# Attention and a mixture of experts on one core: x stored from another queue, a split moved, two scatters moved into a loop

## The chip, the core and the metric

The kernel runs on one core of a Trainium2 chip. A core has five engines with instruction streams of their own: TensorE (PE, matrix products), VectorE (DVE), ScalarE (ACT), GpSimd (POOL) and SyncE (SP, which here only starts transfers), and 16 DMA engines that move data between the main memory and the on-chip memory. Each engine takes its instructions in order and waits on semaphores. The metric is the device time of one launch in microseconds (us), lower is better. A comparison of two kernels rests on their medians.

## The reference

Four batches of 5056 tokens with 256 channels go through an attention over channels (a 256 x 256 matrix for each batch), and the 20224 rows that come out go through a mixture of eight experts, of which each token takes at most one.

```python
qn = q / (np.linalg.norm(q, axis=1, keepdims=True) + 1e-06)
kn = k / (np.linalg.norm(k, axis=1, keepdims=True) + 1e-06)
s = kn.transpose(0, 2, 1) @ qn / tau          # 256 x 256 per batch
a = np.exp(s - s.max(-1, keepdims=True))
a /= a.sum(-1, keepdims=True) + 1e-09
x = (v @ a).reshape(20224, 256)

do_compute = x @ w_skip > 0                   # the others keep out = x
e_idx = argmax(x @ w_gate); gate_w = its softmax
out = x.copy()
for e in range(8):                            # tokens of expert e
    h = np.maximum(x[e] @ w1[e], 0.0)         # 256 -> 1024
    out[e] = x[e] + gate_w * (h @ w2[e])      # 1024 -> 256
```

Products are taken in a fast 32-bit format (fp32r). To keep the precision, an operand is split in a high part H (a cast, on ACT) and the rest L (a subtraction, on DVE), and the products of the parts are added up.

## The kernel before

**The stages.** The program runs through four stages.

1. From 0 to about 460 us a list of tasks written out by a planner. Tokens come in 16 chunks of up to 1280. "A" tasks load q and k and add up the scores of a chunk (`load_qk`, line 616; `scores`, line 671; squares for the norms, line 642). Behind the fourth chunk of a batch comes its softmax. "B" tasks (`attend`, lines 744 to 746) multiply a chunk of v (loaded by `load_v`, line 622, and split by `split_v`, lines 628 and 633, into vH and vL) with the attention matrix aH, aL; `keep_x` (line 751, ACT) copies each product px to the tile xo, of which there are two; `store` (lines 760 to 763) writes xo to `out`. `logits` and `route` (lines 767 to 823) find the expert and the place of each token and scatter its number into lists (line 826, POOL). "H" tasks run the first seven tiles of 512 tokens of one expert ahead, beside the attention.
2. `small.first()`: one small slot (128 tokens of one expert) is run ahead of the loops, at 461 to 473 us.
3. `large.loop()`: six iterations of two tiles of 512 tokens (lines 425 and on), at 473.7 to 752.6 us. A tile is gathered by token number (`gather_x`, line 204, POOL), goes through both products, and is scattered back into `out` (`scatter_x`, line 209, POOL; `put` calls it). The last two scatters of the last tile are `put_last()`, which stands once at the head of the loop's body, for the iteration before, and once behind the loop.
4. `keep_warm(6)`, some matmuls whose result is not used, and `small.loop()`: four iterations of two small slots (U = 2), at 756.8 to 814 us. Each slot loads 1 MB of w1 (v1r) and 1 MB of w2 (v2r) of its expert, splits w2 (`split_w2`, lines 492 and 493) and works on 128 rows. The last result is scattered behind the loop.

**What sets the order.** In stage 1 each task has an engine, a cost and a due time. The planner runs through time, and for each engine takes the ready task that is due first; what it picks is the order in which the instructions are written, and so the order on each engine. "D" tasks stand for transfers; they too occupy one modelled engine, loads by due time. `store` has two tasks there: "S" 0.06 on ACT, which writes the store, and "D" 3.7, which writes nothing and marks when xo may be taken again by a later chunk's first product.

In stages 3 and 4 the order is written by hand. A loop's body is cut into stages; `through(...)` (`behind` in the large loop) says at which point an engine has done what the stage before it promised, and `tc.stage_boundary()` is where the engines meet. So a part of an iteration on one engine may start only after the others have come through theirs. POOL's part of a small slot is: copy the row numbers `ms`, scatter the result `yo` of the slot before, copy `mc` and `mN` (lines 531 and 532), gather the rows `yg` of the next slot.

**The slot run ahead** is the same function `slot(i, u)` with i None: no stage boundaries, and its order of instructions is the order of the text. The relu of its first product is taken in two halves, g = 0 and 1 (lines 526 and 527, tiles yH and yL). It splits w2 of the other slot (v2s0) in four parts: the first two parts behind both relus, the last two within the second product (lines 543 and 544), at f == 3. Its result yo is taken from the product po at lines 552 and 553 (DVE).

Of the kernel before, what the change touches and what calls it, by code (L numbers as in the profile page):

```python
# [15 lines left out]
ALU = mybir.AluOpType  # L16
# [4 lines left out]
P = 128  # L21
B = 4
N = 5056
C = 256
NCH = 4
J = 10
TB = NCH * J
E = 8
# [115 lines left out]
def attn_moe(ctx: ExitStack, tc: tile.TileContext, q, k, vt, tau, w_skip, w_gate, w1, w2, out):  # L144
    nc = tc.nc
# [62 lines left out]
    def scatter_x(ls, src):  # L208
        i = (G.indirect_dma_start(  # L209
            out=out, out_offset=IndirectOffsetOnAxis(ap=ls[:, 0:1], axis=0),  # L210
            in_=src, in_offset=None, bounds_check=NTOK - 1, oob_is_err=False))
        apart(i, *ROWS)
        return i
# [25 lines left out]
    class Large:  # L239
# [184 lines left out]
        def loop(self):  # L424
            with tc.For_i(0, self.n, 1, iteration_sync="staggered", hint_engines=(mybir.EngineType.PE,)) as i, tc.manual_schedule():
                self.put_last()
                self.take(1)
                self.gather(1)
                load_w(self.ei, i + 1, w1, self.w1r)
                behind(G, SP)  # L430
                self.first(True)
                tc.stage_boundary()
                load_list(self.adi, i + 1, self.lN[:, :8, :], 8)
                load_w(self.ei, i + 1, w2, self.w2r)
                for t in range(4):
                    self.second(0, t)
                    if t == 1:
                        behind(T, S, V, G, SP)
                        self.transposed(1)
                tc.stage_boundary()  # L440
                self.take(0)
                self.gather(0)
                behind(G, SP)
                self.first(False)
                tc.stage_boundary()
                for t in range(4):
                    if t < 2:
                        self.split_w1(2 * t)
                        self.split_w1(2 * t + 1)
                    self.second(1, t, t < 2)  # L450
                    if t == 1:
                        self.transposed(0)
                        behind(T, S, V, G, SP)
            self.put_last()

    class Small:

# [48 lines left out]
        def slot(self, i, u):  # L506

            s = 0 if i is None else i + (u + 1)
            through = behind if i is not None else lambda *e: None
            boundary = tc.stage_boundary if i is not None else lambda: None  # L510
            o = (u + 1) % U
            load_w(self.ei, s + U, w2, self.w2r[u])
            if i is not None:
                G.tensor_copy(self.ls[o], self.lc[o])
                scatter_x(self.ls[o][:, 0, :], self.ob[o])
            through(G)
            for g in range(2):
                ph = psum["h"].tile([P, 512], F32, name="ph")
                for f in range(4):
                    po = ph[:, f * P : (f + 1) * P]  # L520
                    for kb in range(2):
                        fs = slice(kb * F + (4 * g + f) * P, kb * F + (4 * g + f + 1) * P)
                        T.matmul(po, self.w1r[u][:, fs], self.xT[u][:, kb, :], start=(kb == 0), stop=(kb == 1), skip_group_check=True)
                fs = slice(4 * g, 4 * g + 4)
                hH, hL = (h[:, fs, :].rearrange("p f t -> p (f t)") for h in (self.hH, self.hL))
                S.activation(hH, ph, AF.Relu)
                V.scalar_tensor_tensor(hL, ph, 0.0, hH, ALU.max, ALU.subtract)
                if g == 0:
                    through(T, S, V, SP)
            boundary()  # L530
            G.tensor_copy(self.lc[o], self.lN[o])
            G.tensor_copy(self.lN[o], self.lP[o])
            load_w(self.ei, s + U, w1, self.w1r[u])
            load_list(self.adi, s + (2 * U + 1), self.lP[o], 1)
            through(SP)
            gather_x(self.xg[u], self.lN[u][:, 0, :])
            through(G)
            po = psum["o", u % 2].tile([P, 512], F32, name="po")
            for c in range(2):
                self.split_w2(o, c)  # L540
            through(S, V)
            for f in range(NFB):
                T.matmul(po, self.hH[:, f, :], self.w2s[u][:, f, :, :], start=(f == 0), stop=False, skip_group_check=True)
                T.matmul(po[:, :C], self.hL[:, f, :], self.w2s[u][:, f, 0, :], start=False, stop=(f == NFB - 1), skip_group_check=True)
                if f == 3:
                    self.transposed(o)
                    for c in range(2, 4):
                        self.split_w2(o, c)
                if f == 4:
                    through(T)  # L550
            gate = self.lc[u][:, 0, 1:2].bitcast(F32)
            V.scalar_tensor_tensor(self.ob[u], po[:, C:], gate, self.xr[u], ALU.mult, ALU.add)
            V.scalar_tensor_tensor(self.ob[u], po[:, :C], gate, self.ob[u], ALU.mult, ALU.add)  # L553
# [7 lines left out]
        def loop(self):  # L561
            with tc.For_i(0, self.n, U, iteration_sync="staggered") as i, tc.manual_schedule():  # L562
                for u in range(U):
                    if u:
                        tc.stage_boundary()
                    self.slot(i, u)
            scatter_x(self.lc[U - 1][:, 0, :], self.ob[U - 1])


# [183 lines left out]
    def store(d):  # L753
        xo = xos[d]
        b, ch = divmod(d, NCH)
        r0 = b * N + ch * P * J
        r1 = r0 + 64 * J
        later = (lambda i: beside(i, "later", "ahead")) if d >= D0 else lambda i: None
        if ch < NCH - 1:
            later(nc.scalar.dma_start(out[r0 : r0 + P * J, :].rearrange("(p j) c -> p j c", j=J), xo[:, :, :C]))  # L760
        else:
            later(nc.scalar.dma_start(out[r0:r1, :].rearrange("(p j) c -> p j c", j=J), xo[0:64, :, :C]))
            later(nc.scalar.dma_start(out[r1 : r1 + 64 * (J - 1), :].rearrange("(p j) c -> p j c", j=J - 1), xo[64:128, : J - 1, :C]))

    def logits(d):
        lg[d] = pb.tile([P, J, 10], F32, name="lg", bufs=3)
# [69 lines left out]
    def tables(start):  # L836
# [15 lines left out]
            V.tensor_tensor_scan(cum[:, i, :], ones[:, :E], nsl[:, i, :], 0.0, ALU.mult, ALU.add)  # L852
        toti = tab.tile([P, 2], I32, name="toti")
        V.tensor_copy(toti[:, 0:1], cum[:, 0, E - 1 : E])
        V.tensor_scalar(toti[:, 1:2], cum[:, 1, E - 1 : E], 1.0, -1.0, ALU.max, ALU.add)
        addr, widx = [], []
        slots.extend([addr, widx, toti])
        yield
# [120 lines left out]
    for d in range(NC):  # L979
# [18 lines left out]
                sv[0][0].users = [t]  # L998
        sv[1][0].users = [t]
        lgt = read[d] = then("lg", add("V", 0.13, lambda d=d: logits(d), [s], hold=("lg", 3)))  # L1000
        st = then("st", add("S", 0.06, lambda d=d: store(d), [s], nominal["B", d, 4] + 3))
        dma = add("D", 3.7, None, [st], nominal["B", d, 4] + 16.5)
        stored[d] = dma
        g = route(d)
        r = chain(g, ("V", 0.43), deps=[lgt] + ([routed[d - 1]] if d else []))
        r += chain(g, ("S", 0.17), ("V", 0.92), ("V", 0.35), deps=r)
# [189 lines left out]
```

## Time and profile before

| | before |
|---|---|
| three runs | 818.23, 823.17, 825.82 us |
| median | 823.17 us |
| profiled execution | 822.56 us |
| its span on the core | 820.6 us |
| mean granted clock of TensorE | 0.984 |
| data moved | 144.97 MB |

The profile is of one execution. Its span is the time between the first and the last instruction that it shows; 1.96 us of the execution's own time lie around it. In a row of a timeline stand the start in us, the duration, the engine, the line of the kernel, the operation, what it writes and reads, and, in square brackets, how long the engine stood before it and what it then was released by. "q" behind an engine's name is the issue of a transfer. Rows of the table of sizes give for a stretch of time how long each engine was busy, TensorE's granted clock (1.00 is full speed), the share of time in which the DMA engines were busy, and the GB/s that they moved. Queue q1 is that of transfers started by SP, q10 of those started by ACT, q0 of those of POOL.

### The profile page before, as it was taken

To read this page: it belongs to the slowest core of one execution; us is meant where nothing else is said; L and a number is where in the kernel's file an instruction comes from. 1 tells how busy PE (TensorE), PEld (TensorE's weight loads), DVE (VectorE), ACT (ScalarE), POOL (GpSimd) and SP (SyncE) were. 2 spreads that over 40 slices of the span, in tenths; PEclk is the share of its full clock that TensorE was granted. 3 is DMA by queue.
4 is the path that set the end of the run, shared out by engine and by line. 5 is a ranking of instruction groups with operands and counts; after the bars stand their busy time and mean duration, and the time that the engine had idled before them with its cause. 6 is when DMAs were issued, how large, how long until landed. Compare 5 with 4: busy or idle time off the path is not lost. (4 is left out here: it accounts for less than half of the span.)

```text
span 820.6 us, 13438 instructions
## 1 busy us (share of the span) xinstructions
PE 787.3 (96%) x4456; PEld 695.0 (85%) x4456; DVE 514.0 (63%) x1005; ACT 365.8 (45%) x579; POOL 391.9 (48%) x423
## 2 busy tenths in 40 slices
PE   7999999979999999999999899999999999998996
PEld 6889998969998888889887778888888888887886
DVE  4719859969989563546476645646556555644665
ACT  5438657838857233325223333324233333322553
POOL 3000378868787777475576133332334433432333
PEclk9999999989999999999999989999999999999999
DMA  8979889969674151412426641222322141321886
GB/s 322 390 267 333 330 260 339 355 251 363 192 243 131 59 158 51 163 46 86 126 52 216 263 142 51 94 96 92 103 89 103 45 147 51 101 78 33 290 315 239
DMA packets 57834, 144.97 MB, mean 177 GB/s; under 512 B 14820, under 2 KB 35324, under 8 KB 52928
## 3 DMA queue, kind: packets, MB, share of 16 engines
q1 hardware_dynamic: 22464, 100.61, 33.7%
q0 software_dynamic: 13952, 22.97, 8.9%
q10 hardware_dynamic: 21376, 20.85, 8.3%
q8 instruction: 23, 0.38, 0.2%
q14 instruction: 19, 0.16, 0.1%
HBM read 114.80 MB, written 32.06 MB: 179 GB/s over the span
## 5 line engine op out<-in xcount | busy, mean ns | idle before, releaser
L826 POOL DMA_INDIRECT lst<-pay,r_posi x160 | 187.4, 1171 | 158.0 <-DVE r_posi L823 111.0
L209 POOL DMA_INDIRECT out<-xg,lc x76 | 76.5, 1006 | 167.3 <-DVE xg L345 140.0
L671 PE MATMUL s<-qt,kt 128*128 128x256 f32 x640 | 151.6, 388 | 4.3 <-DMA kt<-in_k 4.3
L671 PEld LDWEIGHTS s<-qt,kt 128*128 128x128 f32 x640 | 120.9, 195 | 20.0 <-DMA kt<-in_k 3.7
L338 PE MATMUL po<-w2s,hH 128*128 128x512 f32 x384 | 136.4, 398 | 0.0
L321 ACT ACTIVATE hH<-ph 128x512 fp32r<-128x512 f32 x96 | 57.5, 599 | 128.7 <-PE ph L318 128.7
L339 PE MATMUL po<-w2s,hL 128*128 128x256 f32 x384 | 107.2, 279 | 0.0
L744 PE MATMUL px<-aH,vH 128*128 128x266 f32 x320 | 100.0, 312 | 5.0 <-ACT xo L751 5.0
L322 DVE SCALAR_TENSOR_TENSOR hL<-ph,hH 128x512 fp32r<-128x512 f32 x96 | 66.5, 692 | 59.3 <-ACT hH L321 57.8
L204 POOL DMA_INDIRECT xg<-out,lc x80 | 85.2, 1066 | 30.4 <-issue 18.9
L745 PE MATMUL px<-aL,vH 128*128 128x266 f32 x320 | 92.7, 290 | 0.3 <-DVE aL L728 0.3
L746 PE MATMUL px<-aH,vL 128*128 128x266 f32 x320 | 92.4, 289 | 0.0
L338 PEld LDWEIGHTS po<-w2s,hH 128*128 128x128 f32 x384 | 72.1, 188 | 16.6
L751 ACT COPY xo<-px 128x532 f32<-128x532 f32 x80 | 47.7, 601 | 77.8 <-PE px L746 77.8
L316 PE MATMUL ph<-xH,w1H 128*128 128x512 f32 x192 | 76.2, 397 | 3.2 <-DVE yo L553 3.2
L338 PE MATMUL px<-w2s,hH 128*128 128x512 f32 x224 | 79.1, 396 | 0.0
L317 PE MATMUL ph<-xL,w1H 128*128 128x512 f32 x192 | 75.8, 395 | 0.0
L318 PE MATMUL ph<-xH,w1L 128*128 128x512 f32 x192 | 75.8, 395 | 0.0
L339 PEld LDWEIGHTS po<-w2s,hL 128*128 128x128 f32 x384 | 72.3, 188 | 0.5
L744 PEld LDWEIGHTS px<-aH,vH 128*128 128x128 f32 x320 | 61.2, 191 | 6.8 <-ACT xo L751 5.4
L745 PEld LDWEIGHTS px<-aL,vH 128*128 128x128 f32 x320 | 61.3, 191 | 1.9 <-DVE aL L728 0.6
L339 PE MATMUL px<-w2s,hL 128*128 128x256 f32 x224 | 62.8, 280 | 0.0
(189 smaller groups left out, 1485.1 us busy)
## 6 DMA issues: line engine op xcount, KB each, us to landing
vf<-in_vt SPq DMA_DIRECT2D x32, 640.0 KB, 5.8
qt<-in_q SPq DMA_DIRECT2D x31, 640.0 KB, 7.2
kt<-in_k SPq DMA_DIRECT2D x31, 640.0 KB, 7.9
out<-xo ACTq DMA_DIRECT2D x12, 1280.0 KB, 6.5
v1r<-in_w SPq DMA_DIRECT2D x11, 1024.0 KB, 4.9
v2r<-in_w SPq DMA_DIRECT2D x11, 1024.0 KB, 4.9
w1r<-in_w SPq DMA_DIRECT2D x7, 1024.0 KB, 4.8
w2r<-in_w SPq DMA_DIRECT2D x7, 1024.0 KB, 5.0
```

The lines of the kernel that those rows point to most:

```text
L204: apart(G.indirect_dma_start(out=to, out_offset=None, in_=out[0:n, :], in_offset=IndirectOffsetOnAxis(ap=ls[:, 0:1], axis=0), bounds_check ...
L209: i = (G.indirect_dma_start(out=out, out_offset=IndirectOffsetOnAxis(ap=ls[:, 0:1], axis=0), in_=src, in_offset=None, bounds_check=NTOK - ...
L316: T.matmul(ph, self.w1H[:, fs], self.xH[:, kb, :], start=(kb == 0), stop=False)
L317: T.matmul(ph, self.w1H[:, fs], self.xL[:, kb, :], start=False, stop=False)
L318: T.matmul(ph, self.w1L[:, fs], self.xH[:, kb, :], start=False, stop=(kb == 1))
L338: T.matmul(po, self.hH[:, f, ts], self.w2s[:, f, :, :], start=(f == 0), stop=False, skip_group_check=True)
L339: T.matmul(po[:, :C], self.hL[:, f, ts], self.w2s[:, f, 0, :], start=False, stop=(f == NFB - 1), skip_group_check=True)
L671: T.matmul(sums[b][:, cb, :], kt[:, j % JH, cb * P : (cb + 1) * P], qt[:, j % JH, :], start=(ch == 0 and j == 0 and cb == 0), stop=(ch == ...
L744: T.matmul(px[:, i, :NA], vH[:, kb, js], aH[:, kb, :], start=(kb == 0), stop=False)
L745: T.matmul(px[:, i, :NA], vH[:, kb, js], aL[:, kb, :], start=False, stop=False)
L746: T.matmul(px[:, i, :NA], vL[:, kb, js], aH[:, kb, :], start=False, stop=(kb == 1))
L826: i = G.indirect_dma_start(out=lst, out_offset=IndirectOffsetOnAxis(ap=posi[:, t : t + 1], axis=0), in_=pay[:, t0 + t, :], in_offset=None, ...
```

## The change

Four edits.

1. The stores of x are started by SP and not by ACT. In the planner the small ACT task goes, and the 3.7 "D" task writes the store, at the place in SP's order that the planner finds for it.
2. In the small slot run ahead, the four parts of the split of the other slot's w2 stand ahead of the relus: two ahead of g = 0, two ahead of g = 1. Slots in the loop keep the old places.
3. `put_last()` behind the large loop goes. It stands in the small slots' loop instead, behind the slot u = 0, and so in every iteration; the rows written are the same each time.
4. Since those scatters must run at least once, the small loop's number of slots is raised to at least one beyond the slot run ahead. With these inputs it is not changed by that.

```diff
@@ Large.loop
                     if t == 1:
                         self.transposed(0)
                         behind(T, S, V, G, SP)
-            self.put_last()
@@ Small.slot
                 fs = slice(4 * g, 4 * g + 4)
                 hH, hL = (h[:, fs, :].rearrange("p f t -> p (f t)") for h in (self.hH, self.hL))
+                if i is None:
+                    for c in range(2 * g, 2 * g + 2):
+                        self.split_w2(o, c)
                 S.activation(hH, ph, AF.Relu)
                 V.scalar_tensor_tensor(hL, ph, 0.0, hH, ALU.max, ALU.subtract)
...
             po = psum["o", u % 2].tile([P, 512], F32, name="po")
-            for c in range(2):
-                self.split_w2(o, c)
+            if i is not None:
+                for c in range(2):
+                    self.split_w2(o, c)
             through(S, V)
...
                 if f == 3:
                     self.transposed(o)
-                    for c in range(2, 4):
-                        self.split_w2(o, c)
+                    if i is not None:
+                        for c in range(2, 4):
+                            self.split_w2(o, c)
@@ Small.loop
                     self.slot(i, u)
+                    if u == 0:
+                        large.put_last()
             scatter_x(self.lc[U - 1][:, 0, :], self.ob[U - 1])
@@ store
         if ch < NCH - 1:
-            later(nc.scalar.dma_start(out[r0 : r0 + P * J, :].rearrange("(p j) c -> p j c", j=J), xo[:, :, :C]))
+            later(nc.sync.dma_start(out[r0 : r0 + P * J, :].rearrange("(p j) c -> p j c", j=J), xo[:, :, :C]))
         else:
...
@@ tables
-        V.tensor_scalar(toti[:, 1:2], cum[:, 1, E - 1 : E], 1.0, -1.0, ALU.max, ALU.add)
+        V.tensor_scalar(toti[:, 1:2], cum[:, 1, E - 1 : E], 2.0, -1.0, ALU.max, ALU.add)
@@ the tasks of a chunk
-        st = then("st", add("S", 0.06, lambda d=d: store(d), [s], nominal["B", d, 4] + 3))
-        dma = add("D", 3.7, None, [st], nominal["B", d, 4] + 16.5)
-        stored[d] = dma
+        stored[d] = then("st", add("D", 3.7, lambda d=d: store(d), [s], nominal["B", d, 4] + 16.5))
```

The last chunk of each batch has two stores, the others one: 20 in all, of up to 1280 rows of 1 KB. Line numbers behind the edits shift by two to six.

More of the change, by code (lines that the diff above doesn't have):

```diff
@@ L759, in store @@
         if ch < NCH - 1:
-            later(nc.scalar.dma_start(out[r0 : r0 + P * J, :].rearrange("(p j) c -> p j c", j=J), xo[:, :, :C]))
+            later(nc.sync.dma_start(out[r0 : r0 + P * J, :].rearrange("(p j) c -> p j c", j=J), xo[:, :, :C]))
         else:
-            later(nc.scalar.dma_start(out[r0:r1, :].rearrange("(p j) c -> p j c", j=J), xo[0:64, :, :C]))
-            later(nc.scalar.dma_start(out[r1 : r1 + 64 * (J - 1), :].rearrange("(p j) c -> p j c", j=J - 1), xo[64:128, : J - 1, :C]))
+            later(nc.sync.dma_start(out[r0:r1, :].rearrange("(p j) c -> p j c", j=J), xo[0:64, :, :C]))
+            later(nc.sync.dma_start(out[r1 : r1 + 64 * (J - 1), :].rearrange("(p j) c -> p j c", j=J - 1), xo[64:128, : J - 1, :C]))
     def logits(d):
```

## The prediction

> **What bounds the kernel now.** I read the head of the profile's page first.
>
> ```profile
> span 820.6 us, 13438 instructions
> PE 787.3 (96%) x4456; PEld 695.0 (85%) x4456; DVE 514.0 (63%) x1005; ACT 365.8 (45%) x579; POOL 391.9 (48%) x423
> PEclk9999999989999999999999989999999999999999
> q1 hardware_dynamic: 22464, 100.61, 33.7%
> q10 hardware_dynamic: 21376, 20.85, 8.3%
> ```
>
> TensorE (PE) is busy 787.3 of 820.6 us. The change does not touch the number or order of its instructions, so it can win only from two stocks: the 33.3 us in which PE stands, and stretches in which it is busy at a lower clock (the 8s in the clock row). The first stock by its causes, from the table of PE's waits:
>
> ```profile
> PE px L744 <- ACT xo L751: 5.0, 1, 5.0
> PE s L671 <- DMA kt<-in_k: 4.3, 2, 3.7
> PE ph L316 <- DVE yo L553: 3.2, 1, 3.2
> PE ph L523 <- issue: 1.5, 1, 1.5
> PE px L316 <- ACT xH L284: 1.3, 1, 1.3
> PE m L712 <- ACT r_before L805: 0.6, 1, 0.6
> ```
>
> The columns are total, count, longest. The largest is one wait of 5.0 us. Around it I read ScalarE's (ACT's) timeline and the sizes of clock and DMA share, and the store's landing times:
>
> ```profile
> 148.96 0.55 ACTq L760 DMA_DIRECT2D out<-xo  x1
> ...
> 163.29 0.61 ACT L751 COPY xo<-px 128x532 f32<-128x532 f32 x1 [0.91 <-PE px L746]
> 169.54 0.55 ACTq L760 DMA_DIRECT2D out<-xo  x1
> 170.13 1.26 ACT L628 CAST vH<-vf 128x1280 fp32r<-128x1280 f32 x1 [6.24 <-DMA kt<-in_k]
> 171.47 1.09 ACT L751 COPY xo<-px 128x532 f32<-128x532 f32 x2
> ```
>
> ```profile
> DMA to landing us min/median/max: 5.4/6.2/20.5
> ```
>
> ```profile
> 162.00:164.00 2.00, 2.00 (x19) 2.00 (x18) 2.00 (x3) 0.99 (x2) 1.39 (x3) 1.00 1.03 409
> ```
>
> ```profile
> 172.10:175.50 3.40, 3.40 (x14) 3.31 (x15) 3.16 (x10) 0.79 (x2) 1.03 (x2) 0.50 0.81 261
> 411.00:415.00 4.00, 4.00 (x13) 3.09 (x12) 1.21 (x5) 1.08 (x2) 3.09 (x4) 0.57 0.91 204
> 473.80:479.40 5.60, 5.60 (x13) 4.35 (x14) 1.29 (x2) 1.29 (x3) 1.98 (x2) 0.50 0.67 236
> ```
>
> ACT is free at 163.29 + 0.61 = 163.90, and its next instruction, a store of x, goes out only at 169.54. The table of the tile xo has one landing of 20.5 us; 148.96 + 20.5 = 169.46 is 0.08 before that issue. So I read the wait as: the new store may not be issued until the store of 148.96 has landed, and ACT, in order, holds the copies of px behind it. At 162 to 164 the DMA engines are full (share 1.03, 409 GB/s). The last fence has, as its last three columns, PE's clock, DMA share and GB/s: after the 5.0 us PE is busy 3.40 us at clock 0.50, which loses another 1.7.
>
> **The change part by part.** Sums are against the profiled execution: 822.56 us, of which 820.6 is the span. That is 0.6 below the median of 823.17; the three runs spread from 818.23 to 825.82.
>
> *Stores on SyncE (SP).* SP's row around that store, with buffer numbers: vf, qt and kt are loads, xo_1299 is the store that took 20.5 us, xo_1428 the one that waited. Before:
>
> ```order
> L622 DMA vf_1461<-in_vt 128x1280
> L616 DMA qt_1529<-in_q 128x1280
> L616 DMA kt_1530<-in_k 128x1280
> L616 DMA qt_1584<-in_q 128x1280
> L616 DMA kt_1585<-in_k 128x1280
> L622 DMA vf_1638<-in_vt 128x1280
> ```
>
> After:
>
> ```order
> L628 DMA vf_1460<-in_vt 128x1280
> L766 DMA out_0<-xo_1299 1280x1x256
> L622 DMA qt_1529<-in_q 128x1280
> L622 DMA kt_1530<-in_k 128x1280
> L622 DMA qt_1584<-in_q 128x1280
> L622 DMA kt_1585<-in_k 128x1280
> L628 DMA vf_1637<-in_vt 128x1280
> L766 DMA out_0<-xo_1428 1280x1x256
> ```
>
> The store now stands in one queue with the loads, ahead of five that competed with it. The bytes of a packet differ: 20.85 MB in 21376 packets are about 1 KB, 100.61 MB in 22464 are 4.5 KB, so beside a full load queue the store's queue moves few bytes per turn. In one queue it is served in turn. Its own packets need 4.1 us (below); with the two loads just ahead of it, 0.64 MB each at 409 GB/s and so 3.2 together, I estimate a landing of 8 to 12 us, not 20.5. ACT then never stands on a store. Gain: the whole 5.0 and the 1.7 of half clock behind it, **6.7**; the other end, nothing, is rival B.
>
> What it costs: 20 issues and the store's transfer move ahead of loads. A store of 1280 packets takes 1280/16 packets per engine at 0.083 x 820.6 x 16/21376 = 51 ns, 4.1 us; a load right behind comes that much later at most. SP also waits for xo (163.90 for xo_1428) with loads behind it. Cover: loads are early. PE waits for them twice (4.3 in the table), and both times long before the first store, by the timeline and by the first and last start of the stores:
>
> ```profile
> 3.65 2.07 PE L671 MATMUL s<-qt,kt 128*128 128x256 f32 x4 [3.65 <-DMA kt<-in_k]
> 6.38 47.97 PE L671 MATMUL s<-qt,kt 128*128 128x256 f32 x208 [0.66 <-DMA kt<-in_k]
> ```
>
> ```profile
> L760 ACTq DMA_DIRECT2D out<-xo x12: 541/552/641, 85.9 to 388.5; - x12
> ```
>
> I take 0; the other end is rival C.
>
> Two smaller places have ACT issuing two stores ahead of what PE waits for:
>
> ```profile
> 298.68 1.26 ACT L628 CAST vH<-vf 128x1280 fp32r<-128x1280 f32 x1 [1.32 <-issue]
> ```
>
> ```profile
> 408.47 0.66 ACTq L763 DMA_DIRECT2D out<-xo  x1
> 409.18 0.59 ACT L284 CAST xH<-pt 128x512 fp32r<-128x512 f32 x1 [1.32 <-issue]
> ```
>
> Each pair costs ACT 1.32. At 409 the cast of xH is what PE's 1.3 waits for; I take 1.1 of it and leave 0.2 for DVE, whose half of the split follows. Row 411 to 415 above is 4.00 us at 0.57, a loss of 4.00 x 0.43 = 1.7, which I let go too: **2.8**. The Trainium skill (TensorE: Matmul & The Clock Gate, What's actually happening) gives half rate after at least one idle window of about 3.4 us; by that a wait of 1.3 would not have lowered the clock and 1.7 could not be won here, but this trace shows half clock behind 1.3, so the trace differs and decides. At 298 the pair delays the routing chain that ends in the 0.6 wait of L712: **0.6**.
>
> *The second small slot's w2.* In DVE's row of the slot run ahead (v2s0 is the split weight of the other slot, yL the low half of the hidden layer, yo the result). Before:
>
> ```order
> L527 SCALAR_TENSOR_TENSOR yL_4797<-ph_5049,yH_4796 128x512
> L527 SCALAR_TENSOR_TENSOR yL_4797<-ph_5060,yH_4796 128x512
> L493 TENSOR_TENSOR v2s0_4794<-v2r0_4788,v2s0_4794 128x2x256 x4
> L552 SCALAR_TENSOR_TENSOR yo1_156<-po_5096,mc1_4803,yr1_4791 128x256
> ```
>
> After:
>
> ```order
> L492 TENSOR_TENSOR v2s0_4794<-v2r0_4788,v2s0_4794 128x2x256 x2
> L529 SCALAR_TENSOR_TENSOR yL_4797<-ph_5049,yH_4796 128x512
> L492 TENSOR_TENSOR v2s0_4794<-v2r0_4788,v2s0_4794 128x2x256 x2
> L529 SCALAR_TENSOR_TENSOR yL_4797<-ph_5064,yH_4796 128x512
> L556 SCALAR_TENSOR_TENSOR yo1_156<-po_5104,mc1_4803,yr1_4791 128x256
> ```
>
> Nothing stands between the last matmul and yo any more. In time:
>
> ```profile
> 470.29 0.28 PE L544 MATMUL po<-v2s,yL 128*128 128x256 f32 x1
> ```
>
> ```profile
> 470.44 1.29 DVE L493 TENSOR_TENSOR v2s<-v2r,v2s 128x512 fp32r<-128x512 f32 x2 [0.35 <-ACT v2s L492]
> 471.66 0.48 DVE L552 SCALAR_TENSOR_TENSOR yo<-po,mc,yr 128x256 f32<-128x256 f32 x1
> ```
>
> ```profile
> 465.40 0.60 ACT L526 ACTIVATE yH<-ph 128x512 fp32r<-128x512 f32 x1 [2.38 <-issue]
> ```
>
> PE ends at 470.57; L552 could start there, not at 471.66: **1.0** of PE's 3.2 goes, and the rest (L552, L553 and the entry of the large loop) stays. The casts move into ACT's 2.38 of idle time: two take 1.1, so the first relu is not delayed if the weights have landed. The half clock behind (5.60 at 0.50, 2.8 lost) may stay whole or go whole with a gap of 2.2; I let about a third go: **1.0**.
>
> *The puts.* They leave the place between the loops and enter the small loop. POOL's row, one iteration, before (between its gather and the barrier nothing stands):
>
> ```order
> L532 COPY mN1_4799<-mP1_4801 128x2
> L204 DMA yg0_153<-out_0,mN0_4798 128x256
> L562 ISA
> L514 COPY ms0_4804<-mc0_4802 128x2
> L209 DMA out_0<-yo0_155,ms0_4804 20224x256
> ```
>
> After:
>
> ```order
> L534 COPY mN1_4799<-mP1_4801 128x2
> L204 DMA yg0_153<-out_0,mN0_4798 128x256
> L209 DMA out_0<-xg1_140,lc1_148 20224x256 x2
> L566 ISA
> L513 COPY ms0_4804<-mc0_4802 128x2
> L209 DMA out_0<-yo0_155,ms0_4804 20224x256
> ```
>
> The loop runs four times here, so two puts become eight. At the entry:
>
> ```profile
> 753.80 1.57 PE L1142 MATMUL m<-ones 128*128 128x128 f32 x12 [1.26 <-PEq L425]
> 756.84 3.81 PE L523 MATMUL ph<-yT,v1r 128*128 128x128 f32 x32 [1.47 <-issue]
> ```
>
> ```profile
> 755.83 0.97 POOL L209 DMA_INDIRECT out<-xg,lc  x1 [0.31 <-DMA out<-xg,lc]
> 793.03 0.18 POOL L514 COPY ms<-mc 128x2 int32<-128x2 int32 x1 [0.75 <-DMA out<-yo,ms]
> 795.66 1.00 POOL L209 DMA_INDIRECT out<-yo,ms  x1 [2.44 <-DVE yo L553]
> ```
>
> ```profile
> 796.62 0.48 PE L543 MATMUL po<-v2s,yH 128*128 128x512 f32 x1
> ```
>
> PE finishes keep_warm at 755.37 and starts at 756.84, just behind POOL's second put (756.80): the loop's barrier waits for POOL. Without the puts I take **1.4** off. In the loop, two puts are 2 x (0.97 + 0.31) = 2.6 of POOL ahead of the COPY of 793.03, which then comes at 795.6; POOL has only 2.44 of waiting there to take them in, and the scatter follows the COPY by 0.2 at the least, so it starts between 795.8 and, with a gap like those between its other steps, 796.6; I take 796.4, 0.75 later than 795.66. The barrier behind it opens the second half of the slot for PE, which before started 0.04 before the scatter's end (796.62 against 796.66): there is no slack. So 0.75 an iteration, **+3.0** in four. The bounds come from when the second put lands, which the barrier waits for too:
>
> ```profile
> out<-xg,lc POOLq DMA_INDIRECT x76, 2.4
> out<-yo,ms POOLq DMA_INDIRECT x8, 4.3
> ```
>
> Issued at 793.03 + 1.28 = 794.3, it lands at 796.7 by its own median (no more delay) and at 798.6 by that of the loop's other scatter (2.0 an iteration, 8 in all). Nearest is its own row, so 3.0 stands; the low end is 1.5, if half of it hides. A gain is excluded: work is only added ahead of a barrier.
>
> **Sum:** 6.7 + 2.8 + 0.6 + 2.0 + 1.4 - 3.0 = 10.5. 822.56 - 10.5 = **812.1**. Own range: 807 (puts at 1.5, all of the clock at 470, a little more at the loop's entry) to 817 (puts at 8).
>
> **Rivals.**
>
> *A, half clock stays.* If it hangs on when a gap falls and not on its length, the gaps shrink and slow stretches come at other places: 1.7 + 1.7 + 1.0 are not won, 812.1 + 4.4 = 816.5. For it: 5.0, 3.2 and 1.3 all led to it. Against: behind 5.0 us no gap at all remains.
>
> *B, the landing stays 20 us.* It was full DMA engines (1.03), not the queue, and the wait goes to SP, or to the copy that reuses xo. Then the 6.7 stays: 818.8. The Trainium skill (DMA: Bandwidth & Descriptors, Issuing engines are not separate DMA queues) states this as a rule: transfers share the same engines whoever starts them, and the issuer saves only its issue time. For it: the share of 1.03. Against: the median landing is 6.2, and the slow store's 1 KB packets were in a queue of their own beside loads.
>
> *C, loads behind stores come late.* SP is in order; one or two of them arrive after PE asks, each 4.1 and a half-clock stretch of 1.7: 818 to 824. Against: PE waits for no load after the start.
>
> *D, slower: the puts' landing gates the loop.* If under the loop's loads a put takes as much longer as the slow store did (20.5/6.2 = 3.3 times 2.4 = 7.9 us), issued at 794.3 it lands at 802.2, and all engines wait 5.6 in every iteration: 812.1 + 22.4 - 3.0 = 831.5. It turns slower than before from 3.4 an iteration, a landing of 5.8. For it: no slack. Against: 4.3 for a scatter in the same loop.
>
> **How the numbers follow.** Chances: forecast 0.56, A 0.13, B 0.13, C 0.07, D 0.11. 1% is about what a measurement can tell from no change (the runs spread 0.9%); its bounds are 814.9 and 831.4. Faster by over 1%: 0.56 x 0.85, a third of A, little of B: 0.53. Slower: half of D, 0.06. Same: 0.41. The range, 806 to 822, leaves out D, part of C and the forecast's lowest tail, some 0.2.
>
> **What would show it.** Right: no ACT wait near 164 to 170, no store over some 12 us, the L744 wait gone; SP's loads without a new PE wait on kt, qt or vf; L556 starting within 0.2 of PE's end at 470; PE in the small loop within 0.5 of keep_warm's end; PE's wait before the second half of slot 0 at 0.7 to 1 in each iteration, released by POOL. Wrong: a new wait of L671 for kt, a wait on SP that holds vf, a wait in the loop that ends at a put's landing, or half clock at new places.

## The result and the profile after

The change makes the kernel slower: 826.59 us (median of 20 runs, 820.30 to 831.37) against 818.87 us (median of 20, 815.28 to 825.82), a ratio of 1.0081 with a 95% interval of 1.0057 to 1.0105. Ratios here and below are estimated from the single executions, without those over 1.5% above the fastest of their kernel, and so need not be the quotient of the medians beside them. Forecast were 812.1 us and a range of 806 to 822. The profiled execution of the kernel after took 826.61 us, its span is 825.0 us, 4.4 more than in the one of before (820.6).

The head of the page of the kernel after, the same rows as were shown of before:

```profile
span 825.0 us, 13506 instructions
PE 787.1 (95%) x4456; PEld 695.4 (84%) x4456; DVE 514.3 (62%) x1005; ACT 366.7 (44%) x579; POOL 396.2 (48%) x429
PEclk9999999999999999999999899999999999999998
q1 hardware_dynamic: 43008, 121.32, 42.0%
```

PE does as much as before; queue q1 (SP) now has the 20.7 MB that q10 (ACT) had. The table of PE's waits of the kernel after, where the first row is new:

```profile
PE po L546 <- issue: 11.5, 4, 3.8
PE s L677 <- DMA kt<-in_k: 5.5, 2, 3.9
PE ph L522 <- issue: 2.9, 1, 2.9
...
PE ph L316 <- DVE yo L557: 2.1, 1, 2.1
...
PE po L546 <- ACT yH L528: 1.6, 1, 1.6
...
PE m L718 <- ACT r_before L811: 0.6, 1, 0.6
```

The wait of 5.0 us on L744 is gone, the one for yo is 2.1 and not 3.2, and no new wait for qt, kt or vf appeared (the two for kt stand at the start, before any store). The last row, L712 in before, is the wait whose end was forecast at 0.6: it is still there. What is new stands in the small loop (L546, and L522 with 2.9 instead of 1.5).

PE's order is the same in both kernels, product for product. So the start of the same product in both traces can be taken from each other, which shows where time goes and comes (worked out from all 4456 products; minus is earlier than before):

```text
stretch of the trace of before, and what lies there    forecast   measured
165 to 180    store on ACT, 5.0 us of PE, half clock       -6.7       -7.1
245 to 255    nothing of the change                         0         +1.6
300 to 312    two stores ahead of vH                       -0.6       -1.9
406 to 418    two stores ahead of xH                       -2.8       -2.8
470 to 482    entry of the large loop                      -2.0       -2.2
752 to 761    entry of the small loop                      -1.4       +3.1
761 to 814    the small loop                               +3.0      +15.0
elsewhere                                                   0         -1.4
sum                                                       -10.5       +4.3
```

Up to the end of keep_warm the kernel after is 13.8 us ahead; it loses 18.1 from there on. The execution of before that was profiled (822.56) lay 3.7 above the median of its 20 runs.

The small loop, from the end of keep_warm to PE's last product, first before and then after, as rows of the table of sizes (PE busy, PEld, DVE, ACT, POOL, then clock, DMA share, GB/s):

```profile
755.40:814.00 58.60, 54.28 (x400) 50.08 (x400) 36.07 (x61) 30.70 (x64) 22.97 (x42) 1.00 0.83 292
```

```profile
741.60:818.30 76.70, 60.49 (x401) 55.71 (x400) 36.47 (x61) 31.49 (x64) 33.13 (x48) 0.91 0.69 240
```

58.6 us became 76.7. PE stands 16.2 instead of 4.3, and is busy 6.2 longer at a mean clock of 0.91. One iteration in POOL's timeline of the kernel after, then PE at the same place, then the group of transfers issued between 789 and 790 (the last number is the time from issue to landing):

```profile
787.71 1.14 POOL L209 DMA_INDIRECT out<-xg,lc  x1 [0.69 <-issue]
789.15 0.97 POOL L209 DMA_INDIRECT out<-xg,lc  x1 [0.30 <-DVEq L566]
791.11 0.97 POOL L209 DMA_INDIRECT out<-yo,ms  x1 [0.79 <-POOL ms L513]
795.03 0.19 POOL L533 COPY mc<-mN 128x2 int32<-128x2 int32 x1 [2.94 <-issue]
```

```profile
794.94 0.47 PE L546 MATMUL po<-v2s,yH 128*128 128x512 f32 x1 [3.81 <-issue]
```

```profile
out<-xg,lc POOLq DMA_INDIRECT x1, 5.2
```

The second put is issued at 789.15 and lands at 789.15 + 5.2 = 794.35; 0.6 later PE and POOL go on together. POOL had finished its scatter at 792.08. So it is not POOL's time that PE waits for but the put's landing. The same sum holds in the other iterations: 753.18 + 4.3 and PE at 758.15, 770.33 + 4.8 and PE at 775.71, 807.46 + 5.7 and PE at 813.70, each time 0.6 behind the landing. The scatter of yo, issued behind the puts, could be thought to be what is waited for, since it lands at about the same time in three of the iterations. The first iteration rules it out, where PE goes on at 758.15 and it lands at 755.39 + 4.3 = 759.7 (POOL, PE and the transfer issued between 755 and 757):

```profile
755.39 0.98 POOL L209 DMA_INDIRECT out<-yo,ms  x1 [0.79 <-DVE yo L557]
758.15 0.47 PE L546 MATMUL po<-v2s,yH 128*128 128x512 f32 x1 [1.59 <-ACT yH L528]
out<-yo,ms POOLq DMA_INDIRECT x1, 4.3
```

This is the second half of the slot u = 1; the prediction's list of signs calls it slot 0.

Behind three of these waits PE runs at half clock for 3.4 us, as in this row:

```profile
775.50:779.00 3.50, 3.29 (x11) 2.94 (x12) 1.29 (x2) 1.08 (x2) 2.25 (x3) 0.51 0.39 119
```

### The profile page after: what moved, and what is told of

It is laid out like the page before. It is cut to its first block, busy times and chain, and to the rows that moved or that the text cites. A ratio compares the mean times of both kernels' runs of the same rounds, so it can differ in the third digit from the quotient of the medians.

```text
span 825.0 us, 13506 instructions
## 1 busy us (share of the span) xinstructions
PE 787.1 (95%) x4456; PEld 695.4 (84%) x4456; DVE 514.3 (62%) x1005; ACT 366.7 (44%) x579; POOL 396.2 (48%) x429
## 5 line engine op out<-in xcount | busy, mean ns | idle before, releaser
L832 POOL DMA_INDIRECT lst<-pay,r_posi x160 | 184.1, 1151 | 154.7 <-DVE r_posi L829 108.3
L209 POOL DMA_INDIRECT out<-xg,lc x82 | 83.7, 1021 | 162.7 <-DVE xg L345 138.9
L677 PE MATMUL s<-qt,kt 128*128 128x256 f32 x640 | 149.5, 384 | 5.6 <-DMA kt<-in_k 5.5
L677 PEld LDWEIGHTS s<-qt,kt 128*128 128x128 f32 x640 | 118.9, 192 | 21.1 <-DMA kt<-in_k 4.4
L204 POOL DMA_INDIRECT xg<-out,lc x80 | 82.9, 1036 | 30.0 <-issue 19.2
L344 DVE SCALAR_TENSOR_TENSOR xg<-po,lc,xg 128x256 f32<-128x256 f32 x48 | 23.2, 484 | 62.1 <-PE po L339 51.3
```

Of the source, the lines that this page charges most:

```text
L204: apart(G.indirect_dma_start(out=to, out_offset=None, in_=out[0:n, :], in_offset=IndirectOffsetOnAxis(ap=ls[:, 0:1], axis=0), bounds_check ...
L209: i = (G.indirect_dma_start(out=out, out_offset=IndirectOffsetOnAxis(ap=ls[:, 0:1], axis=0), in_=src, in_offset=None, bounds_check=NTOK - ...
L677: T.matmul(sums[b][:, cb, :], kt[:, j % JH, cb * P : (cb + 1) * P], qt[:, j % JH, :], start=(ch == 0 and j == 0 and cb == 0), stop=(ch == ...
L832: i = G.indirect_dma_start(out=lst, out_offset=IndirectOffsetOnAxis(ap=posi[:, t : t + 1], axis=0), in_=pay[:, t0 + t, :], in_offset=None, ...
```

## The experiments

Three sets of runs were made, each on a chip of its own and beside runs of before there. On the chips of the first and the third set the kernel before takes 902.12 and 913.70 us, and PE stands for up to 13 us a time in the straight-line part between 100 and 560 us, from a cause that I did not find; ratios there are wide, and I read those traces by stretch. In the second set before takes 820.88 us.

**Set 1. The puts back behind the large loop (edits 1 and 2 alone).** Against the kernel after:

```diff
@@ Large.loop
+            self.put_last()
@@ Small.loop
-                    if u == 0:
-                        large.put_last()
```

(Edit 4, which only edit 3 needs, is taken back with it.)

> The kernel after, with the two scatters of the last large tile back behind the large loop (edits 1 and 2 alone). Theory: the two traces run 13.75 us apart in favour of the kernel after until the end of keep_warm (755.37 against 741.62), and all of the loss is in the small loop, through the puts. Then this kernel is faster than before by 7 to 14 us (0.985 to 0.991 of before, since the wait of 5 us in the trace of before need not be in each of its runs), and in the small loop PE waits for no landing. Rival: the small loop is slow for another reason that edits 1 or 2 bring (code placed differently, half clock): then the loop still takes over 75 us from the end of keep_warm and the time is not below that of before by 1%.

893.02 us, ratio 0.9932 (0.9886 to 0.9978): faster, and by less than the theory has it. In the trace the small loop takes 59.9 us, and PE waits for no landing in it, so the loop's loss is gone; the size came out in set 2.

**Edit 1 alone** (stores started by SP, planner's task as in the change; the rest as before).

> The kernel before with edit 1 alone: stores of x started by SyncE. Theory: the waits behind ACT's store issues go, 5 to 10 us off, ratio 0.988 to 0.994. Rival: the 20.5 us landing was an accident of the one profiled execution of before; then only the 1 to 3 us of the smaller places go, ratio 0.996 to 0.999.

894.36 us, ratio 0.9994 (0.9945 to 1.0043). By the time alone the rival is right here. By its reason it is not: at the stretch of the long landing, the same products of PE as above, less their start in the trace of before, move like this in the traces (us, from 165 to 180 of that trace):

```text
stores on ACT:  edit 3 -0.2   edit 2 -1.7, 0.0   pad on before +0.4
stores on SP:   after -7.1   edits 1, 2 -7.0, -7.1   edit 1 -7.1, -7.1   pad, edits 1, 2 -7.1
```

On every chip edit 1 wins 7 us there against the trace of before. On this one the other stalls of stage 1 sum up to over 70 us by its end, and the gain is not seen in the time: 7 us would be a ratio of 0.992, below the interval, so by the times a part of it is lost again. Where is not settled. In the next stretch, 180 to 245, the four traces of sets 1 and 3 with stores on SP lose 0.6 (this kernel), 3.2, 7.1 and 8.3 us, where the four with stores on ACT lose under 0.5. So on these chips it is not excluded that loads come late behind stores (rival C); the traces from there hold no landing of loads or stores by which it could be told.

**Edit 3 alone** (puts in the small loop, with edit 4, which they need; the rest as before).

> The kernel before with edit 3 alone: the two scatters in the small loop, in every iteration. Theory: the small loop grows by 16 to 19 us as in the kernel after (waits of 3.5 to 3.8 us in three iterations and 1.6 in one, three or four stretches of half clock of 3.4 us each, and a slower entry), ratio 1.018 to 1.023. Rival: a part of the loss comes from the other edits (the loop starts at another time, the code stands elsewhere): then under 12 us, ratio below 1.014.

916.76 us, ratio 1.0142 (1.0022 to 1.0261): the interval takes in both theory and rival, but the trace decides. The small loop takes 76.2 us from keep_warm's end, against 58.6 in before and 76.7 in the kernel after: all of the growth inside the loop comes with this edit. PE's first wait in this kernel's table:

```profile
PE po L542 <- issue: 14.6, 4, 4.0
```

The entry of the loop, though, was not slower here but faster: a gap of 0.30 us. That part of the theory fell.

This kernel has its stores on ACT and so also tells whether the long landing was an accident of one execution. ACT's timeline, and PE's:

```profile
158.12 0.56 ACTq L761 DMA_DIRECT2D out<-xo  x1
...
178.48 0.55 ACTq L761 DMA_DIRECT2D out<-xo  x1
179.08 1.26 ACT L629 CAST vH<-vf 128x1280 fp32r<-128x1280 f32 x1 [6.30 <-DMA kt<-in_k]
```

```profile
181.05 0.59 PE L745 MATMUL px<-aH,vH 128*128 128x266 f32 x1 [5.09 <-ACT xo L752]
```

The same store, the same wait, PE's 5.09 against 5.03. This trace holds no landing of the store, but the next one is issued 20.4 us behind it, against 20.6 in before. In the three other traces with stores on ACT (edit 2 alone, twice, and the pad on the kernel before, all below) PE's wait is 3.58, 5.23 and 5.36; in the nine with stores on SP there is none. The long landing belongs to the order of before, on every chip on which that order was traced.

**Edit 2 alone** (the split ahead of the relus, the rest as before).

> The kernel before with edit 2 alone: the second slot's w2 split ahead of the relus in the slot run ahead. Theory: the gap of 3.2 us at the entry of the large loop shrinks to 2.1 to 2.2 and one stretch of half clock of 3.4 us behind it goes, 2.7 us in all, ratio 0.996 to 0.998. Rival: the second stretch of half clock stays, 1.0 us, ratio 0.999. A second look at the stores started by ACT as well: theory, one of them takes over 15 us again and PE waits over 3 us for it; rival, none does.

901.93 us, ratio 1.0029 (0.9969 to 1.0088): too wide. In the trace the gap at the entry of the large loop is 2.1 us, as in the kernel after. What its stores show stands above.

**Set 2. POOL's time without a landing.**

```diff
@@ Small.loop (the kernel of the first experiment)
                     self.slot(i, u)
+                    if u == 0:
+                        for t in range(3):
+                            G.memset(large.xg[2], 0.0)
```

> The kernel of the first experiment (puts behind the large loop) with three clears of an unused tile on POOL (0.97 us each in the trace, 2.9 in all) where the loop's puts stood in the kernel after, and no transfer there. Theory: what costs 17 us in the loop is that the barrier waits for the second put's landing, not POOL's 2.6 us of issuing; then from the end of keep_warm to PE's last product the loop takes 58.6 us plus at most 0.75 x 4, so under 63, and PE waits under 1.5 us an iteration at the second half of slot 1. Rival: POOL's time is the cost; then PE waits 3 us or more there in three of four iterations and the loop takes over 70.

810.04 us, ratio 0.9841 (0.9799 to 0.9883), the same as without the clears (0.9859, the next experiment). In POOL's timeline the clears take 3.0 us at the puts' place:

```profile
766.85 1.06 POOL L204 DMA_INDIRECT yg<-out,mN  x1 [0.63 <-issue]
767.90 3.00 POOL L574 MEMSET xg<- 128x1024 f32 x3
770.85 0.19 POOL L514 COPY ms<-mc 128x2 int32<-128x2 int32 x1
771.85 1.00 POOL L209 DMA_INDIRECT out<-yo,ms  x1 [0.82 <-DMA yg<-out,mN]
```

and PE's waits inside the loop are 2.1 us in all. The loop takes 64.8, over the 63 that I set, but its entry gap is 4.8 and not 1.5, and of a stretch of half clock there (6.8 us) 5.9 lie behind it and cost 3.0; without this excess it is 58.5, as before. The rival is out: POOL has room for 3 us an iteration.

**The first experiment's kernel once more.**

> The kernel of the first experiment once more (edits 1 and 2, puts behind the large loop), for its time where the runs of before scatter less. Theory: 6 to 12 us below before, ratio 0.985 to 0.993; all of what the kernel after lost is in the loop's puts. Rival: the fetch of code at the loop's entry and the half clock behind it take back half of the gain, ratio 0.993 to 0.997.

809.85 us against 820.88, ratio 0.9859 (0.9827 to 0.9891): 11 us faster than before. The small loop in its trace, in a row of the table of sizes:

```profile
740.00:798.00 58.00, 54.52 (x401) 50.15 (x400) 36.00 (x61) 30.58 (x64) 24.19 (x42) 1.00 0.83 295
```

So edits 1 and 2 together do about what was forecast for them (6.7 + 2.8 + 0.6 + 2.0 = 12.1), and edit 3 takes it away and more.

**Code that stands elsewhere.** Twelve keep_warm matmuls ahead of everything, where PE waits for its first load:

```diff
         ran = plan.run()
+        keep_warm(12)
```

> The kernel of the first experiment with twelve matmuls of keep_warm's kind at the very start of PE's stream, where PE waits 3.65 us for its first load, so that all later code of PE stands 48 instructions (3 KB) further on. Theory: in five traces PE's entry of the small loop is late (2.7 to 4.9 us after keep_warm, where before has 1.5 and the third experiment 0.3) because a block of 16 KB of PE's code is fetched only then (at most 0.4 us before keep_warm's end, or behind it; in the two others 4.7 us before); moved by 48 instructions the block is fetched before keep_warm, the entry gap falls to 0.3 to 1.5 us and the half clock behind it goes, so 3 us less than the first experiment's kernel. Rival: the gap is the barrier of the loop itself, and stays at 2.7 or more wherever the code stands.

805.26 us, ratio 0.9791 (0.9761 to 0.9822): 4.6 us less than the kernel without them, and the fastest of all. Its six runs lie between 803.81 and 806.60, those of the other between 806.29 and 812.03. The two traces do not show the difference: in both the code was there in time, and the gap is 1.45 and 1.47. That the other runs of the kernel without the twelve had it late is inferred. The matmuls also do something that the expectation left out: with them the first products of the scores follow each other every 0.22 us, without them the first dozen or so every 0.43, which is the pace of half clock. By the 208th product that is worth 0.4 us (it starts at 52.50 and 52.88 us in the two traces), since PE waits for kt in between in both. What the loop's entry does in all traces is worked out from the transfers of kind "instruction" on queue q8 (16 KB each, PE's code) and from the duration of the branch at the head of the loop in PE's queue:

```text
kernel             puts ahead   q8 fetch, us from    branch   gap before PE's
                   of the loop  keep_warm's end      us       first product, us
before             yes          -4.7                 0.47     1.47
edits 1, 2 (set 2) yes          -4.7                 0.47     1.47
edit 3             no           -4.7                 0.47     0.30
after              no           -0.4                 2.95     2.91
edit 1 (set 1)     yes          -0.4                 1.67     2.67
edit 1 (set 3)     yes          +1.4                 3.69     4.76
edits 1, 2 (set 1) yes           0.0                 2.03     3.02
edit 2 (set 1)     yes          +1.9                 3.89     4.89
edit 2 (set 3)     yes          -0.4                 1.93     2.92
POOL's clears      yes          +1.4                 3.77     4.84
empty scatters     yes          +1.4                 3.83     4.92
pad, edits 1, 2    yes          in the large loop    0.37     1.45
pad, before        yes          in the large loop    0.36     1.43
pad, after         no           in the large loop    0.35     0.26
```

In all eight rows with a late fetch the branch ends 1.5 us behind the fetch's end, whenever that is. Where the code is there, the entry takes 1.4 to 1.5 us behind the puts and 0.3 without them; where it is fetched late, 2.7 to 4.9. The two rows of edits 1 and 2 are the same kernel, so it changes from run to run, or from chip to chip; in the three kernels with the pad (the twelve matmuls) it was in time.

**Scatters that write nothing.**

```diff
@@ Small.loop (the kernel of the first experiment)
                     self.slot(i, u)
+                    if u == 0:
+                        for t in range(2):
+                            scatter_x(self.nowhere, large.xg[1][:, 2 + t, :])
```

The tile `nowhere` holds numbers out of range.

> The kernel of the first experiment with two scatters in the loop, at the place where the kernel after has its puts, whose row numbers are all out of range, so that they write nothing (the true puts stand behind the large loop). POOL's time and the wait of the barrier are those of the kernel after, no bytes move. Theory: a landing is mostly a fixed time, so it is still 3 us or more and the loop takes 68 to 76 us from the end of keep_warm to PE's last product. Rival: the 128 KB that each put moves beside 300 GB/s of loads make the landing long; without them it lands within 2 us and the loop takes under 64.

823.79 us, ratio 1.0022 (0.9993 to 1.0052), 14 us more than without the scatters. The loop takes 78.0 us, 2 over the theory's 76, of which its late entry (4.9 and not 1.5) is 3.4, and POOL and PE stand as in the kernel after:

```profile
791.28 1.21 POOL L209 DMA_INDIRECT out<-xg,nowhere  x1 [0.30 <-issue]
793.48 0.98 POOL L209 DMA_INDIRECT out<-yo,ms  x1 [0.79 <-POOL ms L516]
797.40 0.18 POOL L536 COPY mc<-mN 128x2 int32<-128x2 int32 x1 [2.94 <-issue]
```

```profile
797.31 0.76 PE L549 MATMUL po<-v2s,yH 128*128 128x512 f32 x1 [3.24 <-issue]
```

The barrier opens 6.0 us after the issue of an empty scatter. The rival, that the bytes make the landing long, is out. What makes it long is not shown.

**Set 3. Edit 1 alone once more.**

> The kernel before with edit 1 alone (stores of x started by SyncE), once more where the runs of before scatter less. By products of PE that stand at the same place of both orders, the trace of the kernel after gains 6.9 us at the wait of 5.0, 1.3 at 303 and 3.1 at 409 and loses 1.7 to a stretch of half clock at 249: theory, edit 1 alone gives 9 to 11 us, ratio 0.986 to 0.990. Rival: in runs without a profile the long landing is rarer, and it gives under 4 us, ratio above 0.995.

915.35 us, ratio 0.9964 (0.9922 to 1.0006), so not the theory's 0.986 to 0.990 on this chip. Its 7.1 us at the stretch of the long landing are in the list above; in this trace, of an execution of 922.36 us, 8.3 are lost in the stretch behind it, and an entry gap of 4.8 us takes 3.3 more.

**Edit 2 alone once more.**

> The kernel before with edit 2 alone (second small slot's w2 split ahead of the relus), once more. Theory: 2.5 us at the entry of the large loop (1.1 of gap and one stretch of half clock of 1.7 lost, by the trace of the kernel after), ratio 0.996 to 0.998. Rival: the later or earlier fetch of code at the small loop's entry takes it back or adds to it by 3 us, so the ratio is 1.000 or 0.993.

915.14 us, ratio 0.9989 (0.9948 to 1.0031): open. The late fetch was there (2.9 us of entry gap), but its part cannot be told from the time.

**The pad on the kernel before.**

> The kernel before with twelve matmuls of keep_warm's kind at the start of PE's stream and nothing else changed. Theory: they hide in PE's wait of 3.65 us for its first load; their only other effect is that the code of the small loop's entry is there in time in every run. The profile of before had it in time, so the entry gap stays 1.5 us there; over many runs it gives 0 to 2.5 us, ratio 0.997 to 1.000. Rival: the matmuls at the start themselves win or cost something, over 3 us in either direction.

913.31 us, ratio 0.9994 (0.9961 to 1.0028). The matmuls themselves cost or win nothing that could be measured in the time here; the entry gap is 1.43 us.

**The pad on the kernel after.**

> The kernel after with the same twelve matmuls at the start. Theory: the entry gap of 2.9 us falls to 0.5 or less, since neither puts nor code are waited for there, the half clock behind it goes, and 3 to 4.5 us are won against the kernel after (ratio to before 1.003 to 1.006); the waits for the puts' landing in the loop stay at 3.5 us. Rival: the entry gap is the loop's own barrier and stays; then the ratio stays at 1.008.

933.48 us, ratio 1.0219 (1.0174 to 1.0264): neither 1.003 to 1.006 nor 1.008, on a chip where edits 1 and 2, each alone, were not seen to gain anything clear of the noise. By the trace the theory holds: the gap at the entry, and PE's wait in the loop:

```profile
846.49 1.69 PE L522 MATMUL ph<-yT,v1r 128*128 128x128 f32 x13 [0.26 <-issue]
```

```profile
PE po L546 <- issue: 15.4, 4, 4.1
```

With code in time the entry is won as forecast (0.26 against 1.43), and the puts' landing costs what it cost before.

## Why the prediction was wrong

**The stores: right.** 6.7 forecast, 7.1 measured. The longest landing in the kernel after, from the table of the tile xo, is

```profile
DMA to landing us min/median/max: 5.4/6.6/11.3
```

where 8 to 12 was estimated and 20.5 was before. Rival B and the rule of the Trainium skill that it rests on (DMA: Bandwidth & Descriptors, Issuing engines are not separate DMA queues) say that the issuer does not matter beyond the issue time. Here the move did more than that: the same 1280 rows landed after 20.5 us in a queue beside the loads, and after at most 11.3 in line with them. Whether it is the queue, or the place ahead of five loads that came with it, was not taken apart. Loads behind stores came in time in this trace (rival C out; on the chips of sets 1 and 3 it stays open).

**The smaller places: right in sum, in part by luck.** 470: 2.0 and 2.2. The wait is 2.1 to 2.3 in every trace with edit 2 and 3.1 to 3.4 in every one without; DVE's result now starts 0.03 behind PE's last product:

```profile
459.08 0.48 DVE L556 SCALAR_TENSOR_TENSOR yo<-po,mc,yr 128x256 f32<-128x256 f32 x1 [1.70 <-PE po L547]
```

409: 2.8 and 2.8. PE's wait of 1.26 goes in every trace with stores on SP, and stays at 1.26 to 1.28 in the four others with stores on ACT. But in those four no half clock follows it, so the 1.7 behind it in before was not there to be won in every run, and that it went is not the edit's doing alone. 303: 0.6 forecast, 1.9 measured, and by another way. The wait on L712 is 0.63 in all fourteen traces, so that reading of the prediction failed; what goes in the traces with stores on SP is a wait of 0.56 on L282 just behind it. The rest is a stretch of half clock that I had left out, and it hangs little on the edit: it is gone in two traces with stores on ACT, and there in two with stores on SP. One such stretch came up at a new place (239.7, behind a wait of 1.65 that in before had none): +1.6. That much of rival A was true: when a wait falls counts, not only how long it is.

**The step that failed: "Nearest is its own row, so 3.0 stands".** The price of the puts in the loop was sized at 0.75 us an iteration. That was for POOL's time alone, and the 3.0 us of clears show that POOL's time costs nothing there. With a landing of 2.4 us, the median that the table of 76 puts gives, the landing added nothing. But 50 of the 76 stand in the large loop and behind it, where the DMA engines move some 90 GB/s (292 in the small loop), and none in the small loop itself; the scatter of yo, which does stand there, had 4.3, and I had it in hand as the upper end. Measured for the second put of each iteration were 4.3 to 5.7, with a median of 5.0. For the iteration shown: the second put goes out 3.43 us after the gather's start (3.09 forecast), lands 5.2 later, and 0.6 passes until PE goes on; before, PE went on 5.4 after the gather's start. 3.43 + 5.2 + 0.6 - 5.4 = 3.8, which is the wait. The 0.6 was not in my sum either.

**The second half of the same step:** half clock. I priced it at each place where a wait was to go, and not where one was to come. Behind the waits of 3.6 to 3.8 came three stretches of 3.4 us in the loop, 1.4 to 1.7 lost in each. So of the 15.0 lost behind the loop's entry, where +3.0 was forecast, 10.4 are PE standing (13.3 us instead of 2.8) and 4.6 half clock. Rival D, with this mechanism and this place, had said that it turns slower than before from 3.4 an iteration. Its estimate, 831.5, was nearer than the forecast, its chance of 0.11 too low; but that it came so near is partly luck, for its landing of 7.9 was too long and it priced no half clock. What I held against it (4.3 for the other scatter) was a landing at which the gain was already gone: by the sum above 3.43 + 4.3 + 0.6 - 5.4 = 2.9 an iteration, 11.7 in four, and 4.6 of half clock, against the 13.5 forecast elsewhere.

**The entry of the small loop: right in its mechanism, overtaken by another.** The puts did hold it up: with code in time the gap is 1.43 to 1.47 with them, 0.26 to 0.30 without them. But POOL's puts were not all that held it; in this execution PE's branch took 2.95 us for code that was fetched at keep_warm's end, and the first products ran at half clock: +3.1 where -1.4 was forecast. Nothing in the page of before shows this, since there the code had come 4.7 us earlier.

Not settled: why the fetch is early in some runs of the same kernel; and why a scatter takes 5 us in the loop when nothing is written. What edits 1 and 2 give each by itself where before takes 820 us was not timed; it is judged by stretches of the traces.

## What to carry to other kernels

A transfer that is put into a loop cut by barriers may be paid for at its landing, as it was here, and not at its issue; it is to be priced with the landing of transfers in that very loop. Each new wait also has to be asked what clock comes behind it, just as each wait that goes. A small saving (here 1.2 us, once) is not to be bought with work that is repeated in every iteration.

## What the runs showed of the hardware

A scatter of which nothing is written holds the barrier as long as one that moves 128 KB (6.0 us from issue to PE going on, against 5.8).

Code of PE that was fetched late cost 1.2 to 3.4 us at a loop's entry (2.7 to 4.9 against 1.5), the branch ending 1.5 us behind the fetch each time. 48 more instructions at the start of the stream, hidden in a wait, took 4.6 us off the median; some 0.4 of it would be the faster start.

Half clock comes in stretches of 3.41 us or a multiple, but for the last one, which the end of the span cuts. In the trace of before they start at 169.16, 305.69 and 411.51 us, which are 40.0 and 31.0 times 3.413 apart. That agrees with the Trainium skill (TensorE: Matmul & The Clock Gate, What's actually happening), which has a free-running window of 3413 ns. But the rule there that it takes an idle window of that length does not hold here: half clock followed waits of 1.65 and 1.3 us. Nor is such a wait enough: behind the same wait of 1.65 it came in the kernel after and not in before, and behind the one of 1.3 in one of the five traces that have it.
